# Staging batch 1's sums of q and k in another buffer, and issuing six small copies from ScalarE's queue

## The chip, the cores and the metric

The kernel runs on one core of a Trainium2 chip. The metric is the device time of one execution in microseconds (us). Engines are called by their names: TensorE (PE, with its weight loads PEld), VectorE (DVE), ScalarE (ACT), GpSimd (POOL) and SyncE (SP). Transfers are issued from the queues of SP, ScalarE and GpSimd.

## The reference

Attention over q, k and v of 4 batches, 8 heads, 576 tokens and 64 dimensions gives an x of 2304 rows by 512, and two feed-forward networks follow. The attention is a sum of two parts: full attention over q, k and v that are averaged over groups of 4 tokens, and local attention over a band of 7 tokens.

```python
q_d = q.reshape(B, H, Sd, factor, D).mean(axis=3)   # k_d, v_d alike; factor = 4
out_up = np.repeat(sm_attn(q_d, k_d, v_d), factor, axis=2)
mask = np.abs(pos[:, None] - pos[None, :]) < factor
out_local = softmax(where(mask, scale * q @ k.T, -1e9)) @ v
x = rows(out_up + out_local)                          # 2304 x 512
x = (silu(x @ w_gate) * (x @ w_val)) @ w_out          # d_ff 1536
h = x @ w2_in
return (h * clip(h + 3, 0, 6) / 6) @ w2_out           # d_ff 2048
```

## The kernel before

The rows of x are worked on in 5 blocks of 8, 6, 8, 8 and 6 groups. A block runs 68 units of 12 matmuls each, in a list that is fixed when the program is built: G (gate), V (value) and O (out) of the first network, then H and P of the second. The weights come as 64-bit words. In block 0 they are loaded raw by SP (line 219), decoded by ScalarE (line 236) and DVE (line 245), stored decoded in DRAM from ScalarE's queue (`kept`, line 251), and split into a high and a low part by ScalarE (line 263) and DVE (line 268). Later blocks load the decoded ones. A raw load needs one of four buffers, and so waits for the decoding of an earlier unit.

Batch 0's attention comes ahead of the units: this is the front, `first_batch()`. Its order on each engine is written out by hand in the string FRONT, whose steps are issued in that order; each engine and each queue works its own steps off one after the other. The steps that matter here, each with a number from 0 to 5 for a group of 96 tokens: SC (scores on TensorE), M (maxima on DVE), W (exponentials on ScalarE into `held`, a buffer with the tag x2), N (normalization on DVE, in `held`), PT (transposes of `held` on TensorE), Pa and Pd (their eviction to `turned` by ScalarE and DVE), V (values on TensorE, from `turned` and `vw`), Xh and Xl (high and low part of x on ScalarE and DVE). dS to dN are the down-sampled attention; dN writes its result, `odN`. The buffers `vw` hold 102 rows of v for each group of 96 tokens, and 24 more rows that are copied from `odN`, so that V adds the two parts of the attention in one product. `od` issues these six copies (`join_od`, line 141 in the profile), and V waits for the copy of its own group.

For batch 1 the sums of q and k over 4 tokens are made by GpSimd: `two` waits with a small copy for M3's result and issues four loads of the first two of every four tokens (`pairs(0)`, line 703) into buffers with the tag fnat, which batch 0's q and k had; `sums` issues four loads that add the other two tokens (`pairs(2)`), and then four additions (line 716) into `dnq` and `dnk`. TensorE transposes these (line 336: `pqT`, `pkT`) behind units 9, 11, 13 and 15 of block 0.

The pool of the front is closed after it, and its memory is used by the pool of the local attention of batches 1 to 3, whose chunks of q, k and v SP loads (line 141) between the weight loads. The tag x2 is used after the front for the result of the first network and for the output.

Of the kernel before, what the change touches and what calls it, by code (L numbers as in the profile page):

```python
# [11 lines left out]
F32 = mybir.dt.float32  # L12
F32R = mybir.dt.float32r
# [9 lines left out]
P = 128  # L23
# [23 lines left out]
Tq01 Tq00 Eq00 Eq01 Rq0 Tk00 Tk01 Ek01 Tq10 Ek00 Rk0 Tq11 Tk11 dS0 Eq10 Ek11 Eq11 Rq1 Tq20 Tk10 Eq20  # L47
Tk20 Tq21 dM0 Ek10 Ek20 Rk1 dE0 Tq31 Eq21 Tq30 Tk21 Tk31 Eq31 Tk30 dS1 Rq2 Eq30 Ek21 Ek31 Ek30 Rq3
SC0 dM1 M0 Rk3 dE1 Rk2 dT0 dP0 W0 SC1 dS3 dM3 dT1 dP1 SC2 M1 dE3 W1 dS2 dT3 N0 dM2 dP3 SC3 dE2 dT2
PT0 M2 to0 N1 M3 two dP2 to1 de0 Pd0 W3 dO0 dO3 dN0 dN3 dO2 N3 dO1 Pa0 W2 dN2 dN1 od sums to2 PT1  # L50
Pa1 Pd1 SC5 SC4 M5 W5 PT3 V1 M4 N2 Pa3 de1 Xh1 W4 V0 Xh0 Pd3 Xl1 N5 PT2 V3 Pd2 Pa2 Xl0 hi0 PT5 Xh3
N4 Pd5 Pa5 Xl3 to3 V2 Xh2 PT4 de2 Xl2 Pd4 Pa4 de3 V5 lo0 Xh5 V4 Xh4 Xl5 Xl4 hi1 to4 lo1
"""


# [1 line left out]
def tile_kernel(  # L57
# [12 lines left out]
    nc = tc.nc  # L70

    B, H, S, D = q.shape
# [5 lines left out]
    NJH = NJ // 2  # L78
    W = 7
    NC = DM // P  # L80
    F1 = w_gate.shape[1] // P
    F2 = w2_in.shape[1] // P
    UT = 4 * NSEG
# [4 lines left out]
    UMAX = max(BLOCKS)  # L88
# [6 lines left out]
    sp = ctx.enter_context(tc.tile_pool(name="sp", bufs=2))  # L95
# [15 lines left out]
    consts = cp.tile([P, SMALL // 4], F32, name="consts")  # L111
# [27 lines left out]
    def late(eng, dst, src):  # L139

        tc.keep_in_program_order(eng.dma_start(dst, src))  # L141
# [172 lines left out]
    def down_sums(b, kinds, gate=None):  # L314
        if gate is not None:
            tc.keep_in_program_order(nc.gpsimd.tensor_copy(consts[:gate.shape[0], 60:61], gate))
        for ws in kinds:
            for t in range(4):
                for w in ws:
                    if t == 0:  # L320
                        dn[w] = sp.tile([NJH, 2, H, D], F32, tag="dn" + w, name=f"dn{w}{b}", bufs=1)
                    src = {"q": q, "k": k, "v": v}[w]
                    for half in range(2):
                        tok = src[b, :, half * NJH * 4:(half + 1) * NJH * 4, :].rearrange("h (j t) d -> j t h d", t=4)
                        how = {"accum_op": ALU.add} if t else {}
                        tc.keep_in_program_order(nc.gpsimd.dma_start(dn[w][:, half], tok[:, t], **how))
                    yield
# [15 lines left out]
    def down_T(b, dn, qk):  # L343
        for w in "qk":
            qk[w] = sp.tile([P, NC, NJ], F32, tag=w + "dT", name=f"{w}dT{b}", bufs=1)
        for w, hc, pt in sums_T(b):
            nc.scalar.activation(qk[w][:, 2 * hc:2 * hc + 2], pt, AF.Copy, scale=1 / 128 if w == "q" else 1.0)
            yield
# [13 lines left out]
    def first_batch():  # L362

        QT = 96
        WK = QT + 6
        KR = WK + QT // 4
        NT = S // QT
        GT = 6
        TT = S // GT
        with tc.tile_pool(name="fp", bufs=1) as fp:  # L370
# [25 lines left out]
            odN = tmp[:NJH, NC * S:NC * S + 2 * DM].rearrange("p (g e) -> p g e", g=2)  # L396
# [53 lines left out]
            vw = []  # L450
# [17 lines left out]

            def join_od(i):
                half, j = divmod(i * QT // 4, NJH)  # L470
                late(nc.gpsimd, vw[i][WK:KR, i % 2], odN[j:j + QT // 4, half])

            for n in range(4):
                load_vd(n)
# [124 lines left out]
            pw, tot, nm, pT = {}, {}, {}, {}  # L599
# [91 lines left out]
            twos = {}  # L691

            def pairs(t):
                for w, src in (("q", q), ("k", k)):
                    for half in range(2):
                        if not t:
                            st = fp.tile([TT, GT, H // 2, D], F32, tag="fnat", name=f"two{w}{half}", bufs=4)
                            st = st.rearrange("p a h d -> p (a h d)")[:NJH, :2 * H * D]
                            twos[w, half] = st.rearrange("p (h t d) -> p h t d", h=H, t=2)
                        tok = src[1, :, half * NJH * 4:(half + 1) * NJH * 4, :]  # L700
                        tok = tok.rearrange("h (j t) d -> j h t d", t=4)[:, :, t:t + 2]
                        how = {"accum_op": ALU.add} if t else {}
                        tc.keep_in_program_order(nc.gpsimd.dma_start(twos[w, half], tok, **how))

            def two():
                tc.keep_in_program_order(nc.gpsimd.tensor_copy(consts[:QT, 60:61], nm[3][:QT, 0, :1]))
                pairs(0)

            def sums():
                pairs(2)  # L710
                for w in "qk":
                    dn[w] = sp.tile([NJH, 2, H, D], F32, tag="dn" + w, name=f"dn{w}1", bufs=1)
                    for half in range(2):
                        st = twos[w, half]
                        tc.keep_in_program_order(
                            nc.gpsimd.tensor_tensor(dn[w][:, half], st[:, :, 0], st[:, :, 1], op=ALU.add)
                        )

            def od():
                for i in (1, 0, 3, 2, 5, 4):  # L720
                    join_od(i)

            def to(i):
# [9 lines left out]
            def lo(i):  # L733
# [2 lines left out]
            others = {  # L736
                "dS": dS, "dM": dM, "dE": dE, "dT": dT, "dP": dP, "dO": dO,
                "dN": dN, "SC": SC, "M": M, "W": W, "N": N, "PT": PT,
                "Pa": Pa, "Pd": Pd, "V": V, "Xh": Xh, "Xl": Xl, "sums": sums, "two": two,
                "od": od, "to": to, "de": de, "hi": hi, "lo": lo,  # L740
            }
            for step in FRONT.split():
                name, *arg = re.match(r"([A-Za-z]+?)([qk]?)(\d*)$", step).groups()
                if name in ("T", "E", "R"):
                    w, at = arg
# [32 lines left out]
    def values_d(po, par, vd, h, pt):  # L778
        for kh in range(2):
            nc.tensor.matmul(  # L780
                po[par * D:par * D + D], vd[:, kh, h, :], pt[:, kh, :], start=kh == 0, stop=kh == 1
            )

    first_batch()
    front[0] = False

# [302 lines left out]
    for bi in range(NB):  # L1089
# [29 lines left out]
        sums = iter(())  # L1119
        if db:  # L1120
            sums = down_T(db, dn, qk)
            if bi:
                sums = chain(down_sums(db, ["qk", "v"], state["os"][:, (UMAX // 2 - 2) * DM:][:, :1]), sums)
# [69 lines left out]
```

## Time and profile before

| | before |
|---|---|
| median of 3 runs | 959.81 us (959.5 to 960.22) |
| profiled execution, its own time | 959.29 us |
| its span, first to last instruction | 957.6 us |
| TensorE busy | 931.2 us, 97% of the span |
| DVE, ScalarE, GpSimd busy | 730.4, 504.4, 113.7 us |
| mean granted clock of TensorE | 0.990 |

The front takes the first 58 us; the units of block 0 run from there to about 262 us. A row of a timeline gives the start in us, the busy time in us, the engine, the line of the kernel, the operation, what it writes and reads, and in brackets how long the engine was idle before it and what ended that. Line 153 is that of a helper which records the front's operations in order, so there the names of the tiles tell the steps apart: fO is V, fPT is PT, fS is SC.

### The profile page before, as it was taken

The numbers are of one execution on the slowest core, as the hardware profiler recorded it, in microseconds if no ns is written. First come the engines' busy times: TensorE is split into PE (matmuls) and PEld (weight loads), VectorE is DVE, ScalarE is ACT, GpSimd is POOL, SyncE is SP. The second block draws the span as 40 slices with busy tenths as digits, with TensorE's granted clock in tenths as the row PEclk, the third lists the DMA queues.
The fourth block names the chain that finished last, engine by engine and source line by source line (L and its number), as shares of the span: only waits on it lengthen the run. The fifth ranks groups of instructions, "written<-read, shape, count | busy, mean of one in ns | idle before, by whom it ended". The sixth has DMA issues, their size and how long they took to land.

```text
span 957.6 us, 13058 instructions
## 1 busy us (share of the span) xinstructions
PE 931.2 (97%) x4848; PEld 789.4 (82%) x4848; DVE 730.4 (76%) x1066; ACT 504.4 (53%) x942; POOL 113.7 (12%) x124
## 2 busy tenths in 40 slices
PE   8799999999899999999999999999999999999997
PEld 5677888777799978878888778888888888999996
DVE  6689967899879979999755799996347994445652
ACT  4785667876444587553334664443335444444542
POOL 7440012000063200015410000000000000000000
PEclk8999999999999999999999999999999999999999
DMA  9899899586699823359962222453223223433331
GB/s 228 178 255 369 294 334 344 166 263 208 236 285 255 159 89 110 130 180 229 216 137 88 67 67 91 165 205 101 97 90 109 89 88 116 148 133 132 120 123 33
DMA packets 100239, 161.08 MB, mean 168 GB/s; under 512 B 53488, under 2 KB 57200, under 8 KB 100176
## 3 DMA queue, kind: packets, MB, share of 16 engines
q1 hardware_dynamic: 57680, 131.43, 42.5%
q0 software_dynamic: 37600, 11.00, 10.6%
q10 hardware_dynamic: 4896, 17.83, 4.7%
q8 instruction: 38, 0.62, 0.3%
q14 instruction: 25, 0.20, 0.1%
HBM read 137.31 MB, written 22.54 MB: 167 GB/s over the span
## 4 chain that ended last, share of the span: by engine, by line
PE 77%; DVE 11%; DMA 4%; issue 3%; ACT 3%; SPq 1%; POOL 0%; ACTq 0%; DVEq 0%
PE aP L1034 17%; PE pH L357 17%; PE aO L1034 13%; PE pG L357 13%; PE pV L357 12%; DVE wr L268 3%; DVE pv L876 1%; DMA vw<-tmp 1%; PE pS L930 1%; SPq L141 1%; DMA w<-in_moe_w_gate_dram 1%; DVE xf L905 1%; DMA kept<-w 1%; PE pO L780 1%; ACT held L153 1%
## 5 line engine op out<-in xcount | busy, mean ns | idle before, releaser
L268 DVE TENSOR_TENSOR wr<-w,wr 128x1024 fp32r<-128x1024 f32 x170 | 207.6, 1222 | 117.9 <-ACT wr L263 117.7
L263 ACT ACTIVATE wr<-w 128x1024 fp32r<-128x1024 f32 x170 | 179.6, 1056 | 127.6 <-issue 61.4
L357 PE MATMUL pH<-x,wr 128*128 128x512 f32 (+1 forms) x960 | 214.0, 373 | 0.0
L1034 PE MATMUL aP<-wr,gH 128*128 128x512 f32 x864 | 212.5, 396 | 0.3 <-ACT gH L1009 0.3
L357 PEld LDWEIGHTS pH<-x,wr 128*128 128x128 f32 x960 | 173.6, 189 | 25.2 <-issue 2.7
L1034 PEld LDWEIGHTS aP<-wr,gH 128*128 128x128 f32 x864 | 159.9, 188 | 35.6 <-issue 2.7
L357 PE MATMUL pG<-xr,wr 128*128 128x512 f32 (+1 forms) x720 | 153.7, 368 | 1.7 <-ACT xr L153 1.2
L357 PE MATMUL pV<-xr,wr 128*128 128x512 f32 (+1 forms) x720 | 153.6, 368 | 0.9 <-ACT sl L998 0.9
L1034 PE MATMUL aO<-gV,wr 128*128 128x512 f32 (+1 forms) x720 | 152.7, 368 | 0.0
L357 PEld LDWEIGHTS pG<-xr,wr 128*128 128x128 f32 x720 | 130.9, 188 | 19.1 <-ACT xr L153 1.4
L357 PEld LDWEIGHTS pV<-xr,wr 128*128 128x128 f32 x720 | 130.9, 188 | 18.1 <-ACT sl L998 1.4
L1034 PEld LDWEIGHTS aO<-gV,wr 128*128 128x128 f32 x720 | 130.8, 188 | 16.7
L1007 ACT ACTIVATE h<-pH,consts 128x512 f32<-128x512 f32 (+1 forms) x80 | 51.5, 643 | 63.1 <-PE pH L357 62.6
L1009 ACT ACTIVATE gV<-sl 128x512 fp32r<-128x512 f32 (+1 forms) x60 | 35.0, 584 | 75.4 <-DVE sl L1004 75.4
L998 ACT ACTIVATE sl<-pG 128x512 f32<-128x512 f32 (+1 forms) x60 | 33.3, 554 | 67.0 <-PE pG L357 66.9
L1009 ACT ACTIVATE gH<-h 128x512 fp32r<-128x512 f32 (+1 forms) x80 | 46.9, 586 | 31.0 <-DVE h L1008 30.8
L839 DVE TENSOR_TENSOR pr<-q,k 128x1792 f32<-128x1792 f32 x27 | 54.6, 2021 | 10.1 <-DMA k<-in_k_dram 9.9
L1008 DVE SCALAR_TENSOR_TENSOR h<-h,pH 128x512 f32<-128x512 f32 (+1 forms) x80 | 50.5, 632 | 14.3 <-ACT h L1007 13.5
L236 ACT ACTIVATE top<-w 128x512 f16<-128x512 bf16 x68 | 52.8, 792 | 13.3 <-DMA w<-in_moe_w_out_dram 4.2
L1010 DVE TENSOR_TENSOR gH<-h,gH 128x512 fp32r<-128x512 f32 (+1 forms) x80 | 50.5, 633 | 11.2 <-ACT gH L1009 10.9
L876 DVE TENSOR_TENSOR pv<-sc,v 128x1792 f32<-128x1792 f32 x27 | 54.6, 2023 | 0.5
L245 DVE SCALAR_TENSOR_TENSOR w<-w,top 128x512 int32<-128x512 int32 x68 | 46.8, 702 | 10.5 <-ACT top L236 7.5
(133 smaller groups left out, 757.9 us busy)
## 6 DMA issues: line engine op xcount, KB each, us to landing
w<-kept SPq DMA_DIRECT2D x136, 512.0 KB
kept<-w ACTq DMA_DIRECT2D x34, 512.0 KB
w<-in_moe_w_out_dram SPq DMA_DIRECT2D x28, 512.0 KB
w<-in_moe_w_in_dram SPq DMA_DIRECT2D x16, 512.0 KB
w<-in_moe_w_gate_dram SPq DMA_DIRECT2D x12, 512.0 KB
w<-in_moe_w_val_dram SPq DMA_DIRECT2D x12, 512.0 KB
out_dram<-os SPq DMA_DIRECT2D x16, 256.0 KB
dnv<-in_v_dram POOLq DMA_DIRECT2D x24, 144.0 KB, 7.7
```

What stands on the lines that cost most here:

```text
L236: behind(nc.scalar.activation(halves(top[i % 2], 2, F16)[:, :, 1], h3.bitcast(BF16), AF.Copy))
L245: behind(nc.vector.scalar_tensor_tensor(w32[i // 2][:, i % 2].bitcast(I32), h12, 13, top[i % 2], op0=ALU.logical_shift_right, op1=ALU.bitw ...
L263: behind(nc.scalar.activation(parts[i][:, 0], w32[i // 2].rearrange("p u e -> p (u e)"), AF.Copy))
L268: behind(nc.vector.tensor_tensor(r[:, 1], s, r[:, 0].bitcast(F32), op=ALU.subtract))
L357: nc.tensor.matmul(ps, r[:, a, c], x[:, c, b_, :ps.shape[1]], start=part is HIGH and a == c == 0, stop=part is LOW and c == NC - 1,)
L839: nc.vector.tensor_tensor(pr, qt[:, a:a + SUB, None, :].to_broadcast([P, SUB, W, D]), win(kt, a, SUB), op=ALU.mult)
L876: nc.vector.tensor_tensor(pr, pe[:, a:a + SUB, :, None].to_broadcast([P, SUB, W, D]), win(vt, a, SUB), op=ALU.mult)
L1007: nc.scalar.activation(h, ps, AF.Relu, scale=1 / 6, bias=half1[:, 0:1])
L1008: nc.vector.scalar_tensor_tensor(h, h, 1.0, ps, op0=ALU.min, op1=ALU.mult)
L1009: nc.scalar.activation(g[:, 0, :nt], h, AF.Copy)
L1010: nc.vector.tensor_tensor(g[:, 1, :nt], h, g[:, 0, :nt].bitcast(F32), op=ALU.subtract)
L1034: nc.tensor.matmul(ps, **one, start=f_ == 0 and a == b_ == 0, stop=f_ == nf - 1 and b_ == 1,)
```

## The change

The sums of batch 1 are staged in a buffer with the tag x2 in place of the four with the tag fnat. `two` is gone, and `sums`, which now issues both passes of loads and the additions, stands at the end of FRONT. The copies of `od` are issued from ScalarE's queue in place of GpSimd's, in two steps: od0 (groups 1 and 0) ahead of W5 and od1 (groups 3, 2, 5 and 4) behind it.

```diff
-PT0 M2 to0 N1 M3 two dP2 to1 de0 Pd0 W3 dO0 dO3 dN0 dN3 dO2 N3 dO1 Pa0 W2 dN2 dN1 od sums to2 PT1
-Pa1 Pd1 SC5 SC4 M5 W5 PT3 V1 M4 N2 Pa3 de1 Xh1 W4 V0 Xh0 Pd3 Xl1 N5 PT2 V3 Pd2 Pa2 Xl0 hi0 PT5 Xh3
-N4 Pd5 Pa5 Xl3 to3 V2 Xh2 PT4 de2 Xl2 Pd4 Pa4 de3 V5 lo0 Xh5 V4 Xh4 Xl5 Xl4 hi1 to4 lo1
+PT0 M2 to0 N1 M3 dP2 to1 de0 Pd0 W3 dO0 dO3 dN0 dN3 dO2 N3 dO1 Pa0 W2 dN2 dN1 to2 PT1 Pa1 Pd1 SC5
+SC4 M5 od0 W5 od1 PT3 V1 M4 N2 Pa3 de1 Xh1 W4 V0 Xh0 Pd3 Xl1 N5 PT2 V3 Pd2 Pa2 Xl0 hi0 PT5 Xh3 N4
+Pd5 Pa5 Xl3 to3 V2 Xh2 PT4 de2 Xl2 Pd4 Pa4 de3 V5 lo0 Xh5 V4 Xh4 Xl5 Xl4 hi1 to4 lo1 sums
...
             def join_od(i):
                 half, j = divmod(i * QT // 4, NJH)
-                late(nc.gpsimd, vw[i][WK:KR, i % 2], odN[j:j + QT // 4, half])
+                late(nc.scalar, vw[i][WK:KR, i % 2], odN[j:j + QT // 4, half])
...
                         if not t:
-                            st = fp.tile([TT, GT, H // 2, D], F32, tag="fnat", name=f"two{w}{half}", bufs=4)
-                            st = st.rearrange("p a h d -> p (a h d)")[:NJH, :2 * H * D]
+                            st = stage[0][:, len(twos)]
                             twos[w, half] = st.rearrange("p (h t d) -> p h t d", h=H, t=2)
...
-            def two():
-                tc.keep_in_program_order(nc.gpsimd.tensor_copy(consts[:QT, 60:61], nm[3][:QT, 0, :1]))
+            stage = []
+
+            def sums():
+                st = sp.tile([P, NC, 2, UMAX * UT], F32R, tag="x2", name="stage", bufs=1).bitcast(F32)
+                stage.append(st.rearrange("p c a t -> p (c a t)")[:NJH].rearrange("p (n e) -> p n e", n=4))
                 pairs(0)
-
-            def sums():
                 pairs(2)
...
-            def od():
-                for i in (1, 0, 3, 2, 5, 4):
+            def od(n):
+                for i in ((1, 0), (3, 2, 5, 4))[n]:
                     join_od(i)
```

## Rows read from the trace of the kernel before

**Rows 1.** Chain of waits, 0 to 100 us: start, duration, what.
```profile
10.07 4.72 DMA fnk<-in_k_dram
...
37.91 9.59 DMA vw<-tmp
...
47.54 1.55 PE fO L153 x16
...
51.10 0.56 DVE turned L153
...
57.77 5.78 PE pG L357 x24
...
68.52 8.48 DMA w<-in_moe_w_gate_dram
...
86.56 0.26 PE pqT L336 x4
...
98.12 0.26 PE pkT L336 x4
```

**Rows 2.** Timeline of TensorE, 12 to 100 us.
```profile
39.19 0.83 PE L153 MATMUL fPT<-ident,held 96*102 96x96 f32 x8
45.79 1.55 PE L153 MATMUL fO<-turned,vw 126*64 126x96 f32 x16 [5.78 <-DMA vw<-tmp]
...
53.87 0.83 PE L153 MATMUL fPT<-ident,held 96*102 96x96 f32 x8
...
78.08 3.03 PE L357 MATMUL pV<-xr,wr 128*128 128x512 f32 x12 [0.94 <-ACT sl L998]
```

**Rows 3.** Timeline of GpSimd, 0 to 400 us.
```profile
30.76 1.87 POOL L703 DMA_DIRECT2D twoq<-in_q_dram  x2 [0.52 <-issue]
...
37.37 3.09 POOL L141 DMA_DIRECT2D vw<-tmp  x6 [3.14 <-DVE tmp L153]
43.30 1.45 POOL L703 DMA_DIRECT2D twoq<-in_q_dram  x1 [2.83 <-DMA twok<-in_k_dram]
...
55.60 5.46 POOL L716 TENSOR_TENSOR dnq<-twoq 72x512 f32<-72x512 f32 x2 [6.28 <-DMA twoq<-in_q_dram]
63.95 3.07 POOL L716 TENSOR_TENSOR dnk<-twok 72x512 f32<-72x512 f32 x2 [2.88 <-DMA twok<-in_k_dram]
```

**Rows 4.** Timeline of ScalarE, 25 to 112 us; ACTq is its queue's issue.
```profile
37.44 0.67 ACT L153 ACTIVATE turned<-fPT 102x384 f32<-102x384 f32 x1
...
50.34 0.50 ACT L153 ACTIVATE xr<-fO 128x384 fp32r<-128x384 f32 x1
...
53.54 0.34 ACTq L251 DMA_DIRECT2D kept<-w  x1
...
76.49 1.06 ACT L263 ACTIVATE wr<-w 128x1024 fp32r<-128x1024 f32 x1 [4.14 <-DVE w L245]
```

**Rows 5.** Timeline of SP's queue, 60 to 80 us.
```profile
63.20 0.38 SPq L219 DMA_DIRECT2D w<-in_moe_w_gate_dram  x1
67.04 0.33 SPq L141 DMA_DIRECT2D q<-in_q_dram  x1
...
68.52 0.53 SPq L219 DMA_DIRECT2D w<-in_moe_w_gate_dram  x1
```

**Rows 6.** DMA queues, 25 to 70 us (q0, GpSimd's), then 58 to 83 us.
```profile
q0 software_dynamic: 3776, 2.66, 39.1%
...
q1 hardware_dynamic: 2079, 5.48, 64.9%
q10 hardware_dynamic: 634, 2.29, 22.6%
```

**Rows 7.** Busy by stretch: length, PE, PEld, DVE, ACT, POOL, PEclk, DMA share, GB/s.
```profile
38.00:52.00 14.00, 8.02 (x92) 6.74 (x89) 7.31 (x15) 7.92 (x38) 8.11 (x9) 0.76 1.11 222
54.00:58.00 4.00, 2.70 (x42) 2.17 (x40) 4.00 (x8) 2.51 (x7) 2.40 (x1) 1.00 1.40 231
...
146.00:160.00 14.00, 14.00 (x63) 11.60 (x62) 10.28 (x16) 9.81 (x14) 2.76 (x2) 1.00 1.18 340
```

More of the change, by code (lines that the diff above doesn't have):

```diff
@@ L738, in first_batch @@
                 "dN": dN, "SC": SC, "M": M, "W": W, "N": N, "PT": PT,
-                "Pa": Pa, "Pd": Pd, "V": V, "Xh": Xh, "Xl": Xl, "sums": sums, "two": two,
+                "Pa": Pa, "Pd": Pd, "V": V, "Xh": Xh, "Xl": Xl, "sums": sums,
                 "od": od, "to": to, "de": de, "hi": hi, "lo": lo,
```

## The prediction

> **What bounds the kernel now.** I read the page first, then the chain of waits from 36 to 100 us, then the timelines of TensorE, GpSimd, ScalarE and SP over the same stretch, and last the DMA queues and the busy shares by stretch. TensorE is the bound: once its main loop runs, the chain follows it matmul by matmul. So the change is worth what it does to the few places near the start where TensorE waits. The chain shows two. The first is the end of the front: the chain leaves DVE, passes one GpSimd issue, and then spends 9.59 us in one transfer, the copy of down-sampled rows into the buffers `vw` [rows 1]. TensorE has finished PT3 at 39.19 + 0.83 = 40.02 and starts V1 at 45.79, after 5.78 us of idleness put down to that transfer [rows 2]. V0 waits for another such copy until 47.54; from there the chain runs through PT2 and DVE to the first main matmul at 57.77 [rows 1]. The second place is a weight load issued at 68.52 that takes 8.48 us [rows 1]. It makes DVE and then ScalarE late (ScalarE idles 4.14 us before L263 [rows 4]), and TensorE loses 0.94 us before 78.08 [rows 2]. After that the chain stays on TensorE.
>
> Why was the copy slow? GpSimd's timeline gives the order on its queue: four loads of q and k issued from 30.76, then the six copies from 37.37, then four accumulating loads from 43.30 [rows 1, 3]. The accumulating loads had to wait some 12 us for the first ones to land, so those first loads were still running when the copies came behind them.
>
> **The change part by part.**
>
> *The copies go to ScalarE's queue.* In the new order ScalarE comes to od0 after Pa1, which ends at 37.44 + 0.67 = 38.11 [rows 4]; the data (DVE's dN1) is there, since GpSimd could issue its copies at 37.37 [rows 3]. An issue on ScalarE's queue takes 0.34 us [rows 4], so od0's two are out at 38.45 and 38.8, and W5, next on ScalarE, moves back by up to 0.7 us. Nothing near waits for W5, since PT5 comes far later. od1's four issues cost 4 x 0.34 = 1.4 us after W5; ScalarE then had nothing to do before V1, so they are hidden as long as V1 doesn't start before some 42.5. The landing time on this queue is not shown for so small a transfer. From below it is nothing: V1 then starts when TensorE is free at 40.02, and 5.8 us are won. From above it is the old 9.59 us, which puts V0 where it was, and nothing is won. The nearest row of a hardware queue is the last load of k, 144 KB at the end of a full SP queue: 4.72 us from issue [rows 1]. I take that: V1 at 38.45 + 4.72 = 43.2, a gain of 2.6 us; V0 follows directly after V1's 1.55 us, at 44.75, a gain of 2.8. ScalarE's Xh0 at 50.34 [rows 4] and DVE's Pd2 at 51.10 [rows 1] both hang on these, so the first main matmul moves from 57.77 to about 55.0. **Term: -2.8 us, bounds -5.8 and 0.**
>
> The traffic in front of the copies goes away as well, which the row of before can't separate. The Trainium skill, DMA: Bandwidth & Descriptors, section "Issuing engines are not separate DMA queues", says that transfers started by ScalarE, SP or GpSimd share the same 16 engines and interleave, so another issuing engine saves only issue time. By that rule alone the move would win about the half microsecond of a GpSimd issue, and the sum would come out slightly above 959. The trace shows a wait behind earlier work of one queue, and the rule doesn't speak of that. It is a rival below.
>
> *The sums of q and k start later.* They now need the buffer of x2, whose last readers are PT4's transposes. These end at 53.87 + 0.83 = 54.70 [rows 2], so about 51.9 after the shift; the first issue comes at about 52.2 instead of 30.76. Before, from the first issue to the end of q's two additions it took 55.60 + 5.46 - 30.76 = 30.3 us, and to the end of k's 36.3 [rows 3]. Taken whole, q is ready at 82.5 and k at 88.5. TensorE, in its order, asks for q at 86.56 and for k at 98.12 [rows 1]: 83.8 and 95.3 after the shift. So q just fits and k has 7 us. The old 30.3 us also held the six copies between the two passes, some 4 us, so 78.5 is the other end. Cost taken: nothing. If the loads stretch by a quarter, q comes 6 us late, and every microsecond past 83.8 is a stall of TensorE.
>
> *What the sums leave free.* SP's chunk loads of q, k and v were held until 67.04, when GpSimd's additions (the last starting within 63.95 + 3.07) gave up the old buffers [rows 3, 5]. The weight load behind them on SP's queue went out at 68.52 [rows 5]. Now they can follow the weight load of 63.20 directly, so some 3.5 us earlier relative to TensorE. That would take away the 0.94 us.
>
> *What they collide with.* GpSimd's loads now run from about 52 to 82 us, beside the weight loads, the stores of decoded weights and the chunk loads. From 25 to 70 us their queue used 39.1% of 45 us = 17.6 us of all 16 engines [rows 6]. About 0.3 of its 2.66 MB were the copies, so the sums are some 15.6. From 58 to 83 us, which is 55 to 80 after the shift, the two other queues used 64.9% + 22.6% of 25 us = 21.9 us [rows 6]. Together that is 37.5 us of work in 25, a share of 1.50. Shares above 1 occur, because packets of several queues overlap: 1.40 from 54 to 58, 1.18 from 146 to 160 (beside the sums of v, TensorE without a gap), 1.11 from 38 to 52 [rows 7]. At 1.40 the work takes 26.8 us and is 1.8 late; at 1.18 it is 6.8 late; at 1.11 it is 8.8 late. TensorE absorbs some of it: ScalarE's wait of 4.14 became 0.94, so 3.2 are absorbed [rows 2, 4]. The stall is then 0, 3.6 or 5.6 us. I take 1.8, between the first two, since neither stretch has this mix: the one with 1.40 was nearly all accumulating packets, the other had lighter ones. Less the 0.94 of before that is a loss of 0.9. **Term: +0.9 us, bounds -0.9 and +4.7.**
>
> *The rest.* The gate copy of `two` goes, on an idle GpSimd. The sums of v follow later in block 0 as before. x2's own first use lies behind all of block 0's gated products, long after the additions.
>
> **Sum.** The profiled execution took 959.29 us with a span of 957.6; it is 0.5 below the median of 959.81. 959.29 - 2.8 + 0.9 = **957.4 us**.
>
> **Rivals.**
> - *The freed SP queue is the greater effect, and the copies are quick.* V1 at 41.5 to 42 and no stall at 77: the gain is 4 to 5 us, 954.5 to 955.5. For it: the queue in front of the copies is empty. Against it: the 15.6 us of transfers have to go somewhere.
> - *DMA is the bound from 55 to 82 us.* The weight load that follows the first chunk lands late, at the rate of the stretch from 38 to 52, and q's sums with it. At a net loss of 2.8 us the gain is gone; at 4.7 the kernel is at 961.2; with q's sums another 2 us late it is at 963. It decides from a share below about 1.25. For it: in that stretch all queues together moved 222 GB/s, against 340 from 146 to 160 [rows 7]. Against it: from 146 to 160 both streams ran with TensorE fully busy.
> - *The copies land as late as before.* Then the front doesn't move, and what remains is the collision, mostly hidden because the sums start late while TensorE's need doesn't move: 959 to 960. This is what the skill's rule would give.
>
> **Chances.** Forecast (gain of 0.5 to 3.9 us) 0.45; quick copies 0.15; DMA as the bound 0.25; copies as late 0.15. A measurement of this kernel can tell about 0.2%, 1.9 us, from no change. Of the forecast 0.37 lies below that mark, and 0.08 within it. The quick copies are all faster. DMA as the bound splits into 0.18 slower and 0.07 same. The late copies are same. Together: faster 0.52, same 0.30, slower 0.18. The range is 954.3 to 961.5, which leaves about one in ten on either side; the likeliest case alone is 955.4 to 958.8.
>
> **What would show it.** Right: `vw` copies within 5 us of their issue, V1 near 43, the first main matmul near 55, q's additions done before TensorE comes to the transposes of q, and a gap of TensorE between 70 and 80 us of 1 to 3 us. Wrong: TensorE's gap before V1 unchanged (late copies); gaps before the second pair of G and V units or before the transposes of q that add up to more than the front's gain (DMA as the bound); no gap at all between 55 and 90 (quick copies). I would also be wrong if the chunk loads were still held on SP by some other buffer of the front.

## The result and the profile after

The changed kernel takes 974.09 us (median of 4 runs, 970.18 to 974.63) against 959.72 (4 runs, 959.50 to 960.22) of the kernel before beside it: a ratio of 1.014, with a 95% interval of 1.0113 to 1.0167. It is slower by some 14 us, where 957.4 was forecast in a range up to 961.5. The profiled execution took 970.18 (span 968.4), so it is the fastest of the four; what the others took beyond it no trace shows.

The timeline of TensorE after, which answers to [rows 2] and to the main matmuls of [rows 1]:

```profile
42.36 1.69 PE L153 MATMUL fO<-turned,vw 126*64 126x96 f32 x32 [2.15 <-DMA vw<-tmp]
...
54.49 5.78 PE L357 MATMUL pG<-xr,wr 128*128 128x512 f32 x24 [0.99 <-ACT xr L153]
60.48 5.75 PE L357 MATMUL pV<-xr,wr 128*128 128x512 f32 x24 [0.22 <-ACT sl L998]
66.07 2.88 PE L357 MATMUL pG<-xr,wr 128*128 128x512 f32 x12
79.05 0.38 PE L336 MATMUL pqT<-ident,dnq 72*128 72x72 f32 x1 [10.10 <-POOL dnq L716]
81.36 0.62 PE L336 MATMUL pqT<-ident,dnq 72*128 72x72 f32 x3 [1.93 <-POOL dnq L716]
81.73 4.33 PE L357 MATMUL pG<-xr,wr 128*128 128x512 f32 x12
...
91.34 5.60 PE L1034 MATMUL aO<-gV,wr 128*128 128x512 f32 x24
```

The front did get shorter: the front's step V1 starts at 42.36 instead of 45.79, and the first main matmul at 54.49 instead of 57.77, a gain of 3.28 us. The last figure is not exact to a microsecond: e10 below, with the front of before unchanged, starts its main matmuls at 56.23. Then TensorE stands 12.0 us (10.10 and 1.93) for q's sums, ahead of the second half of the second pair of G units. In [rows 1] the same transposes came behind the first O units, at 86.56.

The wait costs more than its length. The 12 matmuls behind it take 4.33 us, against 2.88 for the 12 ahead of it: the granted clock was 0.54 from 70 to 85 us, near the lower of its two levels (1.2 GHz), and 1.00 (2.4 GHz) from 85 us on. TensorE had stood idle for most of 69 to 81 us. The first O unit starts 10.4 us later than before (91.34 for 80.95), so the 10.9 us that the profiled execution lost are nearly all lost by there.

The chain of waits after shows what these sums waited for:

```profile
52.77 8.23 DMA stage<-in_q_dram
...
62.87 17.12 DMA stage<-in_q_dram
79.98 0.07 issue
80.05 1.27 POOL dnq L716
...
81.36 0.62 PE pqT L336 x3
```

GpSimd's timeline after, against [rows 3]:

```profile
52.77 1.86 POOL L702 DMA_DIRECT2D stage<-in_q_dram  x2 [27.58 <-DVE turned L153]
...
61.29 1.41 POOL L702 DMA_DIRECT2D stage<-in_q_dram  x1 [5.07 <-DMA stage<-in_q_dram]
...
80.05 1.26 POOL L716 TENSOR_TENSOR dnq<-stage 72x512 f32<-72x512 f32 x1 [1.06 <-DMA stage<-in_q_dram]
...
89.05 1.29 POOL L716 TENSOR_TENSOR dnk<-stage 72x512 f32<-72x512 f32 x1 [5.38 <-DMA stage<-in_k_dram]
```

The sums of q end at 81.3 and those of k at 90.3, close to the 82.5 and 88.5 of the prediction. Those of q are not late by the forecast; TensorE asks for them 15 us earlier than it assumed (66.07 + 2.88 = 68.95, for 83.8).

The queues of ScalarE and SP after, against [rows 4, 5], and VectorE's first product of the local attention:

```profile
37.30 1.33 ACTq L141 DMA_DIRECT2D vw<-tmp  x1
...
38.67 0.73 ACTq L141 DMA_DIRECT2D vw<-tmp  x1
...
43.81 0.49 ACT L153 ACTIVATE turned<-fPT 102x384 f32<-102x384 f32 x1 [1.67 <-DMA vw<-tmp]
```
```profile
58.32 0.38 SPq L219 DMA_DIRECT2D w<-in_moe_w_gate_dram  x1
58.88 0.34 SPq L141 DMA_DIRECT2D q<-in_q_dram  x1
59.26 0.51 SPq L141 DMA_DIRECT2D k<-in_k_dram  x1
...
60.35 0.38 SPq L219 DMA_DIRECT2D w<-in_moe_w_gate_dram  x1
```
```profile
71.71 2.03 DVE L839 TENSOR_TENSOR pr<-q,k 128x1792 f32<-128x1792 f32 x1 [6.86 <-DMA k<-in_k_dram]
```

An issue of a copy takes ScalarE's queue 0.73 to 1.33 us, and ScalarE stands behind the last of them. SP's chunk loads are no longer held (58.88 instead of 67.04), but the chunk of k then needs 12 us to land, and VectorE waits for it (6.86 us) with the gated product of unit V1 behind it. (Units of a kind are counted from 0: V1 here is the second V unit of block 0, not the front's step V1.)

The busy shares by stretch (length, PE, PEld, DVE, ACT, POOL, granted clock, DMA share, GB/s) and the DMA queues (52 to 82 us: packets, MB, share), against [rows 6, 7]:

```profile
38.00:52.00 14.00, 11.54 (x130) 9.79 (x126) 10.94 (x22) 10.25 (x43) 0.00 (x0) 0.76 0.43 144
54.00:58.00 4.00, 3.51 (x15) 2.90 (x16) 4.00 (x8) 2.98 (x6) 2.23 (x3) 1.00 1.02 352
55.00:80.00 25.00, 14.12 (x60) 10.82 (x59) 14.60 (x17) 10.67 (x15) 8.33 (x7) 0.82 1.12 294
70.00:85.00 15.00, 4.02 (x13) 3.15 (x14) 9.44 (x9) 1.98 (x3) 4.10 (x3) 0.54 1.22 295
```
```profile
q0 software_dynamic: 3333, 2.33, 49.1%
q1 hardware_dynamic: 1717, 4.57, 45.4%
q10 hardware_dynamic: 547, 1.98, 17.2%
```

The DMA engines' work has moved from the front (a share of 0.43 from 38 to 52 us, 1.11 before) to the first units. From 55 to 80 us the share is 1.12, where by the prediction's sum 1.50 would have been needed to bear everything in time. GpSimd's loads took 49.1% of 30 us, 14.7 us, for 2.33 MB; the two hardware queues moved 6.55 MB in 18.8 us. Byte for byte the loads of the sums cost more than twice the engine time.

### The profile page after: what moved, and what is told of

Read it like the earlier page. It is cut to its first block, busy times and chain, and to the rows that moved or that the text cites. A ratio compares the mean times of both kernels' runs of the same rounds, so it can differ in the third digit from the quotient of the medians.

```text
span 968.4 us, 13032 instructions
## 1 busy us (share of the span) xinstructions
PE 932.7 (96%) x4848; PEld 789.6 (82%) x4848; DVE 730.6 (75%) x1066; ACT 504.2 (52%) x942; POOL 105.5 (11%) x117
## 4 chain that ended last, share of the span: by engine, by line
PE 76%; DVE 13%; DMA 5%; issue 3%; ACT 2%; SPq 1%; POOL 0%; ACTq 0%; DVEq 0%
PE pH L357 16%; PE aP L1034 16%; PE pV L357 13%; PE aO L1034 12%; PE pG L357 12%; DVE wr L268 3%; DMA stage<-in_q_dram 3%; DVE pv L876 2%; DVE xf L905 1%; PE pS L930 1%; DMA w<-in_moe_w_in_dram 1%; DVE h L1008 1%; PE pO L780 1%; DVE pv L880 1%; PE fPT L153 1%
## 5 line engine op out<-in xcount | busy, mean ns | idle before, releaser
L357 PEld LDWEIGHTS pH<-x,wr 128*128 128x128 f32 x960 | 172.8, 188 | 25.8 <-issue 2.9
L839 DVE TENSOR_TENSOR pr<-q,k 128x1792 f32<-128x1792 f32 x27 | 54.5, 2020 | 14.7 <-DMA k<-in_k_dram 14.5
```

Of the source, the lines that this page charges most:

```text
L357: nc.tensor.matmul(ps, r[:, a, c], x[:, c, b_, :ps.shape[1]], start=part is HIGH and a == c == 0, stop=part is LOW and c == NC - 1,)
L839: nc.vector.tensor_tensor(pr, qt[:, a:a + SUB, None, :].to_broadcast([P, SUB, W, D]), win(kt, a, SUB), op=ALU.mult)
```

## Experiments

All kernels here build on the kernel before or after. In the texts on record, "the order" is the order of instructions on TensorE, VectorE and ScalarE as the programs are built. It differs between before and after in more than the diff names: the first transposes of q stand after unit G2 instead of behind the first O units, VectorE's first product stands ahead of the gated product of unit V1, and some weights are decoded in another sequence. These instructions are not held to the order in which the program names them; the program's scheduler places them. In three profiled executions (e1, e14, e22) the granted clock was 0.59 to 0.60 from 25 to 40 us where it was 1.00 in the others (0.82 in e20), and the first main matmul came 4 to 7 us later; why is not shown, and for them only what follows the front is read. In the other traces, too, like fronts differ by 1.5 to 3 us (before 57.77 and e10 56.23, e7 54.62 and e6 57.32).

| kernel | copies on | order | sums' loads | first G | first O | O - G | ratio to before (95%) |
|---|---|---|---|---|---|---|---|
| before | GpSimd | before | from 30.76 | 57.77 | 80.95 | 23.2 | 1 |
| after | ScalarE | after | from 52.77 | 54.49 | 91.34 | 36.9 | 1.0140 (1.0113, 1.0167) |
| e10 | GpSimd | pinned | early | 56.23 | 78.17 | 21.9 | 1.0002 (0.9986, 1.0018) |
| e2 | ScalarE | after | early | 58.57 | 86.69 | 28.1 | 1.0061 (1.0039, 1.0083) |
| e5 | ScalarE | transposes pinned | early | 57.67 | 85.83 | 28.2 | 1.0070 (1.0045, 1.0096) |
| e8 | ScalarE | pinned, product early | early | 57.93 | 81.90 | 24.0 | 1.0023 (1.0002, 1.0044) |
| e1 | ScalarE | transposes pinned | late | 61.11 | 91.94 | 30.8 | 1.0095 (1.0064, 1.0127) |
| e6 | ScalarE | pinned, product early | late | 57.32 | 85.98 | 28.7 | 1.0100 (1.0077, 1.0123) |
| e7 | ScalarE | pinned | late | 54.62 | 83.42 | 28.8 | 1.0107 (1.0080, 1.0133) |
| e3 | GpSimd | before | late | 54.63 | 82.76 | 28.1 | 1.0037 (1.0012, 1.0063) |
| e21 | GpSimd | before | late, q's alone | 54.26 | 76.72 | 22.5 | 1.0013 (0.9999, 1.0028) |
| e16 | GpSimd | before | behind the copies | 53.58 | 86.73 | 33.2 | 1.0048 (1.0027, 1.0070) |
| e20 | GpSimd | before | q ahead, k behind | 53.80 | 84.25 | 30.5 | 1.0024 (1.0006, 1.0042) |
| e13 | ScalarE | pinned | paced, 85 to 130 | 53.69 | 76.16 | 22.5 | 1.0034 (1.0008, 1.0061) |
| e14 | GpSimd | pinned | paced, 85 to 130 | 58.36 | 80.27 | 21.9 | 1.0032 (1.0008, 1.0055) |
| e12 | ScalarE | pinned | none | 54.54 | 80.35 | 25.8 | 1.0005 (0.9980, 1.0031) |
| e15 | ScalarE | after | none | 54.02 | 80.37 | 26.4 | 1.0002 (0.9979, 1.0025) |
| e18 | GpSimd | before | none | 53.85 | 76.13 | 22.3 | 0.9963 (0.9945, 0.9981) |
| e22 | ScalarE | after | none, no additions | 60.93 | 84.39 | 23.5 | 0.9966 (0.9941, 0.9992) |
| e24 | GpSimd | before | none, no additions | 53.68 | 75.57 | 21.9 | 0.9943 (0.9918, 0.9967) |

First G and first O are the starts of the first main matmul and of the first O unit in each trace; what is lost behind the first O unit shows in the ratio alone.

### Is it the order? (e1, e6, e7)

The first theory was the new order alone. The pins hold the transposes of batch 1 (all three kernels) and VectorE's first product (e6, e7) to the program's order:

```diff
+                        ins = nc.tensor.transpose(...)
+                        if b == 1:
+                            tc.keep_in_program_order(ins)
...
+            if (b, c, a) == (1, 0, 0):        # e6, e7: the first product
+                tc.keep_in_program_order(ins)
```

In e6 the step of the local attention is also moved from unit 6 to unit 3, so that the product stands where it stood before.

> The changed kernel with the four transposes of batch 1's sums pinned behind the unit that they follow in the program, so that the first stands behind O1 again, as before the change. Theory A (the first transposes were drawn ahead to a place where their sums can't be ready): the sums of q are done at about 81.3 us as in the changed kernel, TensorE now asks at about 83, there is no wait at them, and the time is 955 to 958 us. Theory B (the late loads crowd the weight loads, or come too late in any order): TensorE waits 4 us or more between 65 and 90 us for weights or for the sums, and the time is 962 us or more.

> As the run before, but DVE's first product right behind V1's gated product, the place that it had before the change. Theory C: k's chunk still lands at some 72 us, so DVE stands there about 5 us, but with V1's product already done; TensorE waits 2 to 5 us at V2 or V3 and the time is 958 to 962 us, between that of the run with both pins further back and 965. Theory B: 962 us or more.

> The changed kernel with two pins: the first transposes of the sums behind O1 (as in the first run), and DVE's first product of the local attention behind all that DVE has before it in the program, so behind the gated product of V1 and V2. Theory C (the loss is made by the order of the instructions: DVE stands at that product, waiting for k's chunk, with V1's gated product behind it, and TensorE stands at the transposes): both waits are gone, TensorE waits less than 3 us in all between 55 and 100 us, and the time is 955 to 959 us. Theory B (the loads crowd each other, whatever the order): waits of 4 us or more remain, for weights or for the sums, and the time is 962 us or more.

Measured: 969.38, 969.85 and 971.10 us. TensorE's wait for the transposes is gone in all three, and the time falls by only 3 to 4 us of the 14 (0.33% to 0.45% by the ratios, whose intervals overlap that of after). In e1 the product takes its place; timeline of VectorE, then TensorE:

```profile
77.25 2.02 DVE L841 TENSOR_TENSOR pr<-q,k 128x1792 f32<-128x1792 f32 x1 [5.81 <-DMA k<-in_k_dram]
```
```profile
81.67 4.97 PE L359 MATMUL pG<-xr,wr 128*128 128x512 f32 x12 [6.11 <-DVE sl L1006]
```

With both pinned, in e7, the weights come next, by its chain of waits and TensorE's timeline:

```profile
65.05 15.12 DMA w<-in_moe_w_val_dram
80.23 12.49 DMA w<-in_moe_w_out_dram
```
```profile
78.13 5.49 PE L359 MATMUL pV<-xr,wr 128*128 128x512 f32 x12 [3.56 <-ACT sl L1002]
...
98.82 6.50 PE L359 MATMUL pV<-xr,wr 128*128 128x512 f32 x16 [3.42 <-ACT sl L1002]
```

A weight load of 512 KB that took 8.48 us in [rows 1] takes 12 to 15. Here too the lower clock adds to each wait: the 12 matmuls behind the first one take 5.49 us instead of 2.88, at a granted clock of 0.61 from 80 to 85 us. The place of the transposes and of the product alone falls as the cause: it decides mostly which late transfer is waited for first.

### One part of the change alone (e2, e5, e8, e3, e10)

```diff
 # e2: before + copies on ScalarE (od0 ahead of W5, od1 behind it); the sums stay early, in the front's buffers
-                late(nc.gpsimd, vw[i][WK:KR, i % 2], odN[j:j + QT // 4, half])
+                late(nc.scalar, vw[i][WK:KR, i % 2], odN[j:j + QT // 4, half])
 # e5: e2 + transposes pinned.  e8: e2 + both pins, the step at unit 3.  e10: before + both pins
 # e3: after, with the copies on GpSimd at the place of before
```

> The kernel before with only the copies moved to ScalarE's queue; the sums stay in their old buffers and begin as before. The first transposes stand at the early place here too, ahead of G3. Theory A: the sums are done near 61 us, TensorE asks at about 69, so the early place costs nothing, the front ends 3 us earlier, and the time is 955 to 957 us. Theory B says the same, 955 to 957 us, since nothing is late. A third reading, that the early place itself or the other orders that came with it cost time, gives 960 us or more.

> The copies on ScalarE's queue, the sums as before the change, and the first transposes pinned behind O1. Theory A and B: the same 955 to 957 us as with the early place, within 1 us, since the sums are ready in either place. If the early place costs something by itself, this one is faster than that by what it costs.

> Only the copies on ScalarE's queue, the sums early as before, and both pins (transposes behind O1, DVE's first product behind V1's). Theory C: the 6.6 us that the copies alone cost were the order that came with them, so with the order of before the time is back at 959 to 961 us; it is no faster than before, since the copies landed 8.9 us after their issue on ScalarE's queue too. If the copies cost time by themselves (their issues on ScalarE), it stays at 964 us or more.

> The changed kernel with the copies back on GpSimd's queue at their old place; only the sums are staged in x2's buffer and begin late. The first transposes stand behind O1, as before the change. Theory A: the front ends where it did or 1 to 3 us earlier (no loads ahead of the copies), the sums are ready at about 84 us, TensorE asks at 84 to 87, and the time is 957 to 961 us. Theory B: waits for weights or sums of 4 us or more between 65 and 95 us, 963 us or more.

> The kernel before with both pins (transposes behind O1, where they were, and DVE's first product further back). Control for what the pins do by themselves: theory C expects 958 to 960.5 us, since the product's wait for k (2.4 us before) no longer stands ahead of other work, and its place costs nothing else. If DVE runs short of time later in block 0, it is 961 us or more.

Measured: e2 966.54, e5 967.36, e8 963.04, e3 963.05, e10 960.37 us.

ScalarE's queue brings the copies no sooner while the loads stand in front of them. The chain of e2 and ScalarE's timeline:

```profile
37.35 8.89 DMA vw<-tmp
```
```profile
43.23 4.39 ACTq L141 DMA_DIRECT2D vw<-tmp  x2
47.73 0.49 ACT L153 ACTIVATE turned<-fPT 102x384 f32<-102x384 f32 x1 [5.53 <-PE fO L153]
```

The copy takes 8.89 us against 9.59 in [rows 1], V1 starts at 46.28, and ScalarE itself now stands 4.39 us in the issue of the last two. In e3, with the copies on GpSimd and the loads gone from in front of them, the copy takes 6.31 us, V1 starts at 43.72 and the first main matmul at 54.63. So the front's gain belongs to the loads' absence, and to the queue next to nothing (0.14 us between e3 and after at the first main matmul).

Moving the copies also made the new order: the programs of e2 and after have the same order on TensorE, VectorE and ScalarE, those of e3 and before too. By itself the copies' move costs 6 us (e2), and 2 us with the transposes and the product at their old places (e8); pins alone cost nothing (e10). With the loads late the copies' move costs more: after is 1.0% above e3, 9.9 us, and e6, which has the transposes and the product back at their old places, is still 0.6% above it.

E3 has the order of before and still loses. VectorE, then TensorE:

```profile
73.44 2.03 DVE L839 TENSOR_TENSOR pr<-q,k 128x1792 f32<-128x1792 f32 x1 [5.76 <-DMA k<-in_k_dram]
```
```profile
78.30 4.63 PE L357 MATMUL pV<-xr,wr 128*128 128x512 f32 x12 [4.32 <-ACT sl L998]
```

The chunk of k, in e3's chain 12.69 us from issue to landing, holds VectorE; the decodes behind it come late, and with them ScalarE and TensorE.

### The loads taken away (e12, e15, e18, e22, e24)

In e12, e15 and e18 GpSimd fills the stage with zeros instead of loading it, so the sums of q and k are zeros; in e22 and e24 the additions are left out as well, and zeros are written straight into the sums.

```diff
-                pairs(0)
-                pairs(2)
+                nc.gpsimd.memset(stage[0], 0.0)                  # e12 (from e7), e15 (from after), e18 (from e3)
...
+                    tc.keep_in_program_order(nc.gpsimd.memset(dn[w], 0.0))   # e22 (after), e24 (e3): nothing else of sums
```

> As the run with the transposes and the first product pinned (e7, 971 us), instruction by instruction on TensorE, VectorE and ScalarE, but batch 1's eight loads of q and k are left out: GpSimd fills their buffer with zeros, so the sums of q and k are zeros here. Theory of crowding (the loads beside the first weights and chunks make these late): the gate, value and out weights land within 9 us again, no TensorE wait over 2 us between 60 and 100 us, and what stays is the gain of the front, 3.3 us, and the freed SP queue, 0.9: 955 to 958. Rival (the cost lies in the copies on ScalarE's queue, or in the changed order of the decodes that the pins don't mend): still 966 or more. In between, 959 to 965: both, and the split is read off.

> The changed kernel with its own order (transposes of q ahead of G3, first product ahead of V1's gated product), but batch 1's eight loads of q and k left out, the buffer filled with zeros instead, so the sums of q and k are zeros here. Theory of crowding: without the loads the new order has little to wait for; the transposes of q find their input ready, VectorE's first product waits some 2 to 3 us for k; 956 to 961. Theory of order (the new order alone costs some 10 us): 966 or more. The difference to the pinned run beside it is what the order costs without crowding: 0 to 4 us.

> As e3 (stage in x2's buffer, copies on GpSimd at the place of before, order of TensorE, VectorE and ScalarE as before), but batch 1's eight loads of q and k left out: GpSimd fills their buffer with zeros, so the sums of q and k are zeros here. With the order of before and no loads, the first V unit follows the first G unit without a wait, unlike in e12 and e15 (2.01 us and half the clock there). If the order ate the front's gain in those two: V1 at 43 to 44, first main matmul at 54.5, first O unit at 77 to 78 instead of 80.95, 955.5 to 958. Rival (the weights give the pace whatever the order, so that a front that ends earlier only waits for them): the first O unit at 80 to 81 with waits of 2 to 3 us for weights before it, 959 to 961.

> The changed kernel, its order of instructions on TensorE, VectorE and ScalarE unchanged, but batch 1's sums of q and k left out whole, loads and additions: GpSimd writes zeros for the sums early in the front. In e15 GpSimd's additions fell at 55 to 62 us and VectorE's decodes took 1.71 us each there instead of 0.68, so e15 is not a clean reading of the new order. If that was why the front's gain didn't come out: decodes of 0.68, no wait of 2 us before the first V unit, the first O unit at 76.5 to 78, and 955 to 957.5. If the new order itself eats the gain: first O unit at 79 to 81, a wait of TensorE of 1 us or more at the first V unit or at VectorE's first product (for the chunk of k), 959 to 961.

> The same with the copies on GpSimd at the place of before, so with the order of before: batch 1's sums of q and k left out whole, zeros in their place. By both theories as e18 or a little better: first O unit at 76 to 77, 954.5 to 957. The difference to the run beside it is the price of the new order and of ScalarE's queue, without loads or additions: 0 to 1 if only the additions hurt e15, 3 to 5 if the order does.

Measured: 960.94, 960.62, 955.68, 956.60 and 954.69 us. Without the loads some 10 us (e12 against e7) and 13 us (e15 against after) are gone, in whichever order. In e15 the sums are also ready early; in e7 TensorE doesn't wait for the sums, nor in e3 (7.1 us above e18), so e12 against e7 and e18 against e3 show crowding by the loads alone. It is the main cause. But e12 and e15 only come back to the time of before. VectorE, ScalarE and TensorE of e15:

```profile
57.21 5.14 DVE L245 SCALAR_TENSOR_TENSOR w<-w,top 128x512 int32<-128x512 int32 x3
```
```profile
59.02 0.79 ACT L236 ACTIVATE top<-w 128x512 f16<-128x512 bf16 x1 [2.79 <-DVE w L245]
```
```profile
61.77 7.34 PE L357 MATMUL pV<-xr,wr 128*128 128x512 f32 x24 [2.01 <-ACT sl L999]
```

The three decodes take 1.71 us each instead of 0.68, because GpSimd's additions, no longer waiting for loads, run beside them from 54.9 to 61.8. In the new order ScalarE has to pass such a decode before it comes to `sl`, and TensorE waits 2.01 us, and the 24 matmuls of V then take 7.34 us instead of the 5.60 of e18 (the granted clock is 0.89 from 55 to 70 us, 1.00 in e18). In e18 the decodes are as slow (5.18 us for three), but `sl` stands ahead. Without the additions, in e22, all decodes take 0.68 to 0.69, and the gain comes out: 0.9966 beside 0.9943 of e24. What the new order and ScalarE's queue cost by themselves would then be 0.23%, 2.2 us, with intervals that overlap, so this is not clear of noise.

TensorE and the stretch from 70 to 85 us of e24, with no loads of the sums at all:

```profile
53.68 5.73 PE L357 MATMUL pG<-xr,wr 128*128 128x512 f32 x24 [1.21 <-ACT xr L153]
...
75.57 5.61 PE L1026 MATMUL aO<-gV,wr 128*128 128x512 f32 x24
```
```profile
70.00:85.00 15.00, 15.00 (x71) 12.39 (x70) 15.00 (x17) 8.71 (x13) 0.00 (x0) 1.00 1.00 367
```

TensorE has no gap, and still the DMA share is 1.00: weights, decoded stores and chunks fill that stretch without any sums. Loads moved into it come on top of that. A share near 1 is no proof of a stall by itself, though: [rows 7] has 1.18 from 146 to 160 us beside a gapless TensorE.

### Other places for the loads (e16, e20, e13, e14, e21)

```diff
 # e16, before's kernel: two (gate and first loads) goes behind od;  e20: q's first loads stay at two, k's first loads go behind od
 # e13 (from e7), e14 (from e3, pinned): four pairs of loads, each behind a GpSimd copy of an element of a g tile
+            if i in (9, 13, 17, 21, 25):              # the additions at 25; transposes at units 27 to 33
+                pace[0].send(last)
 # e21, from e3: the stage's half of k filled with zeros, so the sums of k are zeros
-                pairs(0)
-                pairs(2)
+                pairs(0, "q")
+                pairs(2, "q")
+                nc.gpsimd.memset(stage[0][:, 2:], 0.0)
```

> The kernel before with one step moved: GpSimd issues the six copies of down-sampled rows first, and then batch 1's four loads of q and k, in the front's own buffers as before; TensorE, VectorE and ScalarE have the order of before, instruction by instruction. If the queue in front of the copies made them slow: V1 starts at 43 to 44 instead of 45.79, the first main matmul at 54.5 to 55.5. The loads then begin at about 40 instead of 30.76, 8 to 10 us later, the additions end at 70 to 75, and SP's chunk loads, held behind them, go out at 73 to 77. Theory of crowding (whatever of these loads falls behind 55 us is paid by the weights): the gain of 2 to 3 us is given back in part, 957 to 962. Rival (only the late start at 52 us of the changed kernel crowds, the stretch from 40 to 70 us has room): 956 to 958.

> The kernel before, with GpSimd's queue in this order: the two first loads of batch 1's q, the six copies, the two first loads of k, then the accumulating loads. Half of the traffic in front of the copies, the other half 8 to 9 us later; TensorE, VectorE and ScalarE have the order of before. Theory (the front and the weights share one stretch of DMA time, so that what the front wins by loads that start later comes back as weights that land later): V1 at 44 to 45, the first main matmul at 56 to 56.5, k's additions 3 to 5 us later than before, chunk loads held until 69 to 71, and 958.5 to 962. Rival (half of the loads find room): 957 to 958.5.

> As e7 with the copies on ScalarE, the stage in x2's buffer, but the eight loads in four pairs, each pair behind a GpSimd copy of one element of a g tile of the main loop (units 9, 13, 17 and 21), the additions at unit 25, and the transposes of q and k at units 27 to 33 in place of 9 to 15, pinned. Theory of crowding: the loads have the stretch from 90 to 130 us to themselves beside the weights, where the share of the DMA engines was 0.86 to 0.92 before; that gives about 1.25 there, with TensorE's weights three units ahead: no wait over 2 us, 955 to 958. If loads of that size cost the same wherever they stand: 962 to 968, with weight loads of 12 us or more at 90 to 130 us.

> As e13, with the copies on GpSimd's queue where they stood before. Theory of crowding: the queue ahead of the copies is empty here, so V1 starts at 43 to 44 as in e3 (43.72) and the front gains 2 to 3 us: 956 to 959, at most 1.5 us behind e13. Rival (ScalarE's queue is what wins the front): V1 at 45 or later, 958 to 961. If paced loads still crowd: 962 or more, like e13.

> As e3 (stage in x2's buffer, copies on GpSimd, order of before), but only the four loads of q; k's half of the buffer is filled with zeros, so the sums of k are zeros here. Half the dose between e18 (no loads, 955.7) and e3 (963.1). Theory of crowding by volume: half the loss, 958.5 to 960.5, with TensorE waits of 2 to 4 us for weights between 70 and 100 us. Rival (the loss comes only once the loads last longer than some slack): 955.5 to 957.5. Rival (any such load beside the first chunk costs it all): 962 to 964.

Measured: e16 964.17, e20 961.88, e13 964.32, e14 964.42, e21 960.58 us. None beats the kernel before.

E16 keeps the order and gives the copies an empty queue: V1 at 42.13 and the first main matmul at 53.58, 4.2 us sooner. But the last load of k, by its chain, takes 17 us, and SP's chunk loads are held until 71.97:

```profile
53.58 17.03 DMA twok<-in_k_dram
```
```profile
81.44 5.49 PE L357 MATMUL pV<-xr,wr 128*128 128x512 f32 x12 [7.09 <-ACT sl L998]
```

E20, with half of them moved, loses half as much. In e13 and e14 nothing is late by 85 us (first O 22.5 and 21.9 us after the first G), and the loss comes behind that. Chain, TensorE and GpSimd of e13:

```profile
101.39 13.15 DMA w<-in_moe_w_val_dram
...
124.08 3.15 DVE sc L861
127.23 3.01 DVE pr L848
```
```profile
132.48 5.49 PE L359 MATMUL pV<-xr,wr 128*128 128x512 f32 x12 [4.65 <-ACT sl L1009]
```
```profile
124.59 3.76 POOL L723 TENSOR_TENSOR dnq<-stage 72x512 f32<-72x512 f32 x2
```

A weight load of 13.15 us stands in the chain, and TensorE's wait of 1.46 us at 116.89 follows from it; so my expectation of quick weights at 85 to 130 us was wrong for e13, at a share of 0.85 to 0.97. But the longest wait of TensorE, 4.65 us, has VectorE ahead of it: `sc` and `pr` take 3.15 and 3.0 us beside GpSimd's additions, where `pr` takes 2.0 elsewhere in this trace and the same `sc` 0.24 in e14. E14's one wait (4.27 us at 128.32) has such VectorE work ahead of it too, at shares of 0.95 to 1.20. Going by e15, the additions, moved to unit 25, bear a part of these losses; but no run has the paced loads without the additions, so this is not shown, and whether the loads alone find room there stays open.

E21's half dose costs 0.5% more than e18, against 0.74% for the full dose of e3; it stops TensorE elsewhere, at the transposes, because the last load of q takes 23.39 us even without k's:

```profile
87.75 0.62 PE L336 MATMUL pqT<-ident,dnq 72*128 72x72 f32 x3 [5.37 <-POOL dnq L721]
```

## Why the prediction was wrong

*The front (-2.8 us).* Measured -3.28, V1 at 42.36 for a forecast 43.2. The size was right, the reason only half, and the landing time of 4.72 us, borrowed from another transfer, came near by luck (5.06 us from od0's issue at 37.30 to V1). The prediction named the queue in front of the copies on GpSimd and took another engine's queue as the cure, though it saw that the traffic in front goes away as well; e2 and e3 show that the traffic counts, whichever queue issues behind it. The Trainium skill, DMA: Bandwidth & Descriptors, "Issuing engines are not separate DMA queues", says that transfers of all issuing engines run interleaved on the same 16 DMA engines and that another issuing engine saves only the time of the issue; e2 agrees (8.89 us for 9.59). The rival built on it failed on the other part of the change, which took the traffic away. The 0.34 us for an issue on ScalarE was also too little: 0.73 to 1.33.

*The sums come late but just fit (0).* The sums came when forecast. The first step that failed is "TensorE, in its order, asks for q at 86.56 ... 83.8 after the shift": it took the order of the instructions that the diff doesn't name as fixed. The new program drew the transposes ahead to 68.95. That is 12.0 us in the trace, but it is not 12.0 us of the result, since e1, e6 and e7 without this wait are only 3 to 4 us better. The prediction also took each microsecond of waiting as one of time; with the lower clock behind it (4.33 us for 12 matmuls instead of 2.88) it is more.

*The freed SP queue (-0.94).* The chunk loads did go out earlier, as said (8 us, 4.9 of them relative to the first main matmul), but into the crowd: the chunk of k takes 12 us.

*The collision (+0.9, bounds -0.9 and +4.7).* This is the second step that failed, the term that was mis-sized. The prediction took a stall of 1.8 us, halfway between those of a share of 1.40, read from a stretch of 4 us that was nearly all accumulating packets, and of 1.18; that is a share of some 1.25. With this mix the share was 1.12, at the lowest of the three that it weighed, 1.11, whose stall of 5.6 us it had as a bound and did not take. And it let TensorE absorb 3.2 us of what was left, although the loads stretched every transfer beside them, weights, chunks and their own second pass. The runs give the loads' price when moved: 1.0037 against 0.9963 with the order of before, 0.74% or 7.1 us (e3, e18), and 10 to 13 us in the new order (e7 against e12, after against e15). The rival "DMA is the bound" had the mechanism, at a chance of 0.25; its sign, gaps before the transposes of q beyond the front's gain, is in the trace, and its 961.2 to 963 is what e3 gives. With the new order on top neither it nor the range reached the result: the ratio is 1.0037 with the loads late in the old order (e3), 0.9966 in the new order without loads and additions (e22), and 1.0140 with both.

What the profile of before could not show, e24 does: the sums already cost some 0.57%, 5.5 us, where they stood (1 against 0.9943). The change saved that 5.5 us and paid about 19 (1.014 against 0.9943). Of that, in the old order, 9 are the loads and additions at their new place (e3 against e24). The other 10 come with the copies' move, beside loads that are late: the changed order and ScalarE standing in its issues. The places of the transposes and the product are 3 to 4 of them, with intervals that overlap (e6, e7); the other order of the decodes and ScalarE's issues were not parted with the loads in place, and what each costs stays open. One gap also stays: the median is 3.9 us above the profiled execution.

## What to carry to other kernels

Before moving a transfer, read the DMA share of the place where it goes in a run without it: here that was 0.85 to 1.01 with next to no gap of TensorE (e18, 55 to 85 us), and the moved loads still cost 7 us, paid by every transfer beside them. The slow copy behind bulk loads was cured by taking the loads away, not by another issuing engine. A wait of TensorE can cost more than its length where the granted clock falls with it: in e15, 2.01 us of waiting and 1.74 us of slower matmuls. And after any change of an engine or a queue, compare the built order of instructions on all engines: those that nothing pins may move.

## What the runs showed of the hardware

- Loads on GpSimd's queue took 14.7 us of all 16 engines for 2.33 MB, the hardware queues 18.8 us for 6.55 MB (after, 52 to 82 us); beside them, 512 KB weight loads went from 8.5 to 12 to 15 us.
- The issue of a 24-row copy inside the chip's memory holds ScalarE 0.73 to 1.33 us, and up to 4.39 us for two (e2) while earlier transfers are under way.
- VectorE's decode of 128x512 words takes 1.71 us beside GpSimd's additions and 0.68 without (e15, e22). The Trainium skill, SBUF — State Buffer, "SBUF: two separate sides", says that VectorE and GpSimd share a pair of ports under an exclusive lock, held for a whole instruction, which a VectorE operation with two SBUF inputs (as the decode) takes against a GpSimd operation that reads SBUF; these rows agree with that.
- While TensorE stood idle for 12 us the granted clock fell: 0.54 from 70 to 85 us, near the lower level of 1.2 GHz, and 1.00 (2.4 GHz) again from 85 us (after). The 12 matmuls behind the wait took 4.33 us instead of 2.88; behind a wait of 3.56 us in e7 they took 5.49.
